# Two fill products between the row scores and the key scores of every step of a fused attention and Fourier kernel

## The chip, the cores and the metric

The kernel runs on one core of a Trainium2 chip. The metric is the device time of one execution in microseconds (us). Before the change three runs gave 2705.79, 2703.69 and 2701.54, with a median of 2703.69. A change within 0.2%, about 5.4 us, is what a measurement of this kernel can hardly tell from none.

## What is computed

```python
def _A_ref(x, wq, wk, wv, wo):          # S = 2048, D = 1024, 32 heads of 32
    q = (x @ wq).reshape(B, S, H, Dh).transpose(0, 2, 1, 3)
    k = x @ wk                          # one key and one value head for all 32
    v = x @ wv
    p = softmax(einsum("bhqd,bkd->bhqk", q, k) * Dh ** -0.5)
    o = einsum("bhqk,bkd->bhqd", p, v)
    return o.transpose(0, 2, 1, 3).reshape(B, S, H * Dh) @ wo

def _B_ref(x, seq_re, seq_im, hid_re, hid_im):
    a, b = x @ hid_re.T, x @ hid_im.T
    return seq_re @ a - seq_im @ b

out = concatenate([_A_ref(...), _B_ref(...)], axis=-1)
```

## The kernel before

The attention is cut into 32 units (four blocks of 512 queries, eight groups of four heads), and each unit into 32 steps. Step n of the main loop (line 940) does two things for attention. `score_step(n + 44)` (line 858) calls `scores` (line 744): two products of 512 columns, the **row scores** of a later unit, go into a tile `pss` (two buffers of two banks). VectorE takes the maximum of each row from it (`nm<-pss`), and in the next step `row_sums` (line 755) has ScalarE write the exponentials back over `pss` and read out their sum. `expo(n)` (line 805) makes two products of 512 columns, the **key scores** of the present unit, in `pst` (one buffer of two banks), and ScalarE writes their exponentials to a tile `p`. In the trace the row scores are `pss<-kst,qst`, the key scores `pst<-qst,kst`.

ScalarE's queue therefore holds, step by step, the row sum of the step before (an ACTIVATE and the READ_ACCUMULATOR) and then the exponential of this step's key scores. As `pst` has one buffer, the key scores of a step can begin only when the exponential of the step before has been read out; as `pss` has two, the row scores of a step need the row sum of two steps before.

All other matrix work (the projections, the Fourier half and the output projection, as three products of split operands each) is a long list of **fill products** `psb<-rh,mh`, `psb<-rl,mh`, `psb<-rh,ml` of 512 columns. `take(n)` (line 379) issues the next n of them; every product that `take` issues also moves the preparation on (`pump` and `run_later`), and the last one of a group (12 or 24 products) has its result taken out of PSUM, mostly by VectorE. Of the 5376 fill products a part runs in the prologue; `goal` (line 926) spreads the rest evenly over the steps, and `level(n)` (line 932) gives each step its share.

Steps 0, 12 and 22 of a unit (`ENDS`) are closed by a **burst**: `pv` (line 819) multiplies the collected `p` tiles by the values, 40 or 48 products `psb<-p,v` with 32 output rows each, four running side by side. `aside` (line 405) first issues up to five fill products when the fill group that is open has only begun or is nearly over. `level` leaves these steps out, and shares the work up to the next burst among the other steps:

```python
        if r in ENDS:
            return
        more = min(e for e in ENDS if e > r) - r
        left = goal(n + more) - pos["fill"]
        take(round(left / more))
```

In the last 44 steps there are no row scores left.

Of the kernel before, what the change touches and what calls it, by code (L numbers as in the profile page):

```python
# [101 lines left out]
def tile_kernel(ctx: ExitStack, tc, xT, wq, wkv, wo, xbT, wT, cT, out):  # L102
# [51 lines left out]
    class Line:  # L154
# [24 lines left out]
        def pump(self):  # L179
            for k in range(4):  # L180
                while self.may(k) and self.items[self.n[k]].due - self.lead[k] <= pos["fill"]:
                    self.step(k)
# [94 lines left out]
    def add(gs):  # L277

        for g in gs:
            i0 = g.at = end[0]  # L280
            end[0] += g.n
            if groups and g.set[0] is not groups[-1].set[0]:
                prev["set"] = prev["this"]
                prev["this"] = i0
            for c, it in enumerate(g.right):
                if it.need is None:
                    it.need = i0 + 3 * c
                    p0 = min(prev["set"], i0 - it.back)
                    it.due = min(it.need, p0 + (i0 - p0) * (g.first + c + 1) // (len(g.set) * len(g.right))) - it.ahead
                    RL.items.append(it)  # L290
                it.last = i0 + 3 * c + 2
            for c, it in enumerate(g.left):
                if it.need is None:
                    it.need = it.due = i0 + 12 * c
                    ML.items.append(it)
                it.last = i0 + 12 * c + 11
            for it in g.ys:
                it.due = i0 + g.n
                ylist.append(it)
            groups.append(g)  # L300
# [14 lines left out]
    def at(p, f):  # L315
        k = len(later)
        while k and later[k - 1][0] > p:
            k -= 1
        later.insert(k, (p, f))

    def run_later():
        while later and later[0][0] <= pos["fill"]:
            later.pop(0)[1]()
# [29 lines left out]
    def bank(name, open_=False):  # L353

        while held:
            held.pop(0)()
        b = 1 - cur["bank"] if cur["bank"] is not None else int(used[1] < used[0])
        cur["at"] += 1
        used[b] = cur["at"]
        if open_:  # L360
            cur["bank"] = b
        return ps_b[b].tile([P, W], F32, name=name)
# [10 lines left out]
    def product(g, ps, j):  # L373
        c, w = divmod(j, 3)
        l, r = g.left[c // 4], g.right[c]
        a = (l.lo if w == 2 else l.hi)[:, c % 4]
        te.matmul(ps[:g.rows], a, r.lo if w == 1 else r.hi, start=j == 0, stop=j == g.n - 1)

    def take(n):
        for _ in range(n):  # L380
            if cur["group"] >= len(groups):
                return
            g = groups[cur["group"]]
            j = pos["fill"] - g.at
            if j == 0:
                cur["ps"] = bank("psb", True)
            if j % 3 == 0:
                RL.force(g.right[j // 3])
            if j % 12 == 0:
                ML.force(g.left[j // 12])  # L390
            product(g, cur["ps"], j)
            pos["fill"] += 1
            if j == g.n - 1:
                cur["group"] += 1
                assert all(hasattr(it, "done") for it in g.ys)
                g.post(cur["ps"])
                cur["at"] += 1
                used[cur["bank"]] = cur["at"]
                cur["bank"] = None
                if g.ys:  # L400
                    at(pos["fill"] + 2 * BEHIND + 5, lambda n=len(g.ys): yused.__setitem__(0, yused[0] + n))
            pump()
            run_later()
# [174 lines left out]
    def wo_set(e):  # L578
        return [Item([(lambda g=g: wo[g * P:(g + 1) * P, e * W:(e + 1) * W], 1)]) for g in range(NG)]
# [90 lines left out]
    def o_group(b, t, e, ws):  # L670
        def post(ps):
            r0 = b * W + t * P
            to = out[r0:r0 + P, e * W:(e + 1) * W]
            if b < NQ - 1:
                oo = op.tile([P, W], F32, name="qh")
                dve.tensor_copy(oo, ps)
                store(to, oo)
                return

            n = len(halves)  # L680
            halves.append(n)
            oo = pp.tile([P, 2, W], F32, name="p")
            if n + 1 < 8:
                if n % 2:
                    dve.tensor_copy(oo[:, 0], ps)
                else:
                    act.activation(oo[:, 0], ps, AF.Copy)
                move(act, to, oo[:, 0])
                return
            for k, q in enumerate((act, sp)):  # L690
                cols = slice(k * W // 2, (k + 1) * W // 2)
                if k:
                    dve.tensor_copy(oo[:, k, :W // 2], ps[:, cols])
                else:
                    act.activation(oo[:, k, :W // 2], ps[:, cols], AF.Copy)
                move(q, to[:, cols], oo[:, k, :W // 2])
        return Group([o_left(b, t, q) for q in range(2)], ws, post)
# [101 lines left out]
    def inverse(u):  # L799
        rb[u] = onp.tile([P, W], F32, name="rb")  # L800
        for h in range(4):
            r = r_d[u][4 * h:4 * h + 4].rearrange("t c -> (t c)")
            sp.dma_start(rb[u][h * DH:(h + 1) * DH], r.unsqueeze(0).to_broadcast([DH, W]))

    def expo(n):
        u, r = divmod(n, SU)
        c, hp_ = divmod(r, 2)
        pt[u, c, hp_] = pp.tile([P, 2, W], F32, name="p")
        ps = ps_t.tile([P, 2, W], F32, name="pst")
        for a in range(2):  # L810
            te.matmul(ps[:, a], kst[:, c * P:(c + 1) * P], qst[u][:, 2 * hp_ + a], start=True, stop=True)
        act.activation(pt[u, c, hp_], ps, AF.Exp)
# [45 lines left out]
    def score_step(s):  # L858

        if s < total:  # L860
            u, r = divmod(s, SU)
            if r == SU - 6 and u + 1 < len(units):
                open_unit(u + 1)
        if SU <= s < SU * (len(units) + 1) and s % SU == TURN:
            row_sums(s - 1)
            lse_3((s - SU) // SU)
        if s < total:
            scores(s)
        row_sums(s - 1)
        u, e = divmod(s - SU, SU)  # L870
        if 0 <= u < len(units):
            for f in LSE.get(e, ()):
                f(u)
# [52 lines left out]
    def goal(n):  # L926
        return PRO + (FILL - PRO - LAST - MORE * (total - QUIET)) * n // total + MORE * max(n - QUIET, 0)
# [4 lines left out]
    def level(n):  # L932
        r = n % SU
        if r in ENDS:
            return
        more = min(e for e in ENDS if e > r) - r
        left = goal(n + more) - pos["fill"]
        take(round(left / more))

    for n in range(total):  # L940
        u, r = divmod(n, SU)
        if n == total - 12:
            w1 = wo_set(1)
            add([o_group(NQ - 1, t, e, ws) for e, ws in ((0, w0), (1, w1)) for t in range(4)])
        score_step(n + SU + LEAD)
        if ends:
            ends.pop(0)()
        expo(n)
        if r == 16:
            inverse(u)  # L950
        if r in ENDS and n:
            pv((n - 1) // SU, (ENDS.index(r) - 1) % (len(CUT) - 1))
        level(n)


    last = groups[len(groups) - 8:]
# [75 lines left out]
```

## Time and profile before

| what | value |
|---|---|
| three runs, median | 2703.69 us |
| the profiled execution's own time | 2701.05 us |
| its span, first to last instruction | 2699.3 us |
| granted TensorE clock, whole span | 1.0 |
| PE busy | 2691.8 us (100%), 13820 products |
| weight loads (PEld) | 1918.1 us (71%) |
| ScalarE | 2134.8 us (79%) |
| VectorE | 1592.8 us (59%) |
| GpSimd | 1723.7 us (64%) |
| DMA traffic | 538.24 MB, mean 199 GB/s |

Times are of one profiled execution; "busy" of PE counts pipelined products from issue to their modelled end, so two products that overlap share their time, and a short wait between products does not show in the share. The start times in the timeline do show it. "Idle before" names what ended a wait.

### The profile page before, as it was taken

The numbers are of one execution on the slowest core, as the hardware profiler recorded it, in microseconds if no ns is written. First come the engines' busy times: TensorE is split into PE (matmuls) and PEld (weight loads), VectorE is DVE, ScalarE is ACT, GpSimd is POOL, SyncE is SP. The second block draws the span as 40 slices with busy tenths as digits, with TensorE's granted clock in tenths as the row PEclk, the third lists the DMA queues.
The fourth block names the chain that finished last, engine by engine and source line by source line (L and its number), as shares of the span: only waits on it lengthen the run. The fifth ranks groups of instructions, "written<-read, shape, count | busy, mean of one in ns | idle before, by whom it ended". The sixth has DMA issues, their size and how long they took to land.

```text
span 2699.3 us, 40577 instructions
## 1 busy us (share of the span) xinstructions
PE 2691.8 (100%) x13820; PEld 1918.1 (71%) x13820; DVE 1592.8 (59%) x1826; ACT 2134.8 (79%) x3131; POOL 1723.7 (64%) x1711
## 2 busy tenths in 40 slices
PE   9999999999999999999999999999999999999999
PEld 6876767676777767677776777667677776767767
DVE  5766666666666666565565656666565555655411
ACT  3588888888888888888888888888888888888741
POOL 4854425777547558765556675576887987865751
PEclk9999999999999999999999999999999999999999
DMA  8543336887788566564354588984675765644665
GB/s 277 190 136 128 114 97 202 282 285 233 241 268 281 203 226 195 175 193 142 125 160 152 183 258 278 306 262 128 213 226 161 223 199 159 209 142 134 192 211 187
DMA packets 316931, 538.24 MB, mean 199 GB/s; under 512 B 35962, under 2 KB 63354, under 8 KB 316666
## 3 DMA queue, kind: packets, MB, share of 16 engines
q1 hardware_dynamic: 315572, 533.69, 61.6%
q8 instruction: 109, 1.79, 0.3%
q10 hardware_dynamic: 1152, 1.97, 0.2%
q14 instruction: 98, 0.80, 0.1%
HBM read 395.58 MB, written 138.15 MB: 198 GB/s over the span
## 4 chain that ended last, share of the span: by engine, by line
PE 99%; ACT 0%; DVE 0%; DMA 0%; SPq 0%; issue 0%; ACTq 0%
PE psb L79 62%; PE pss L79 19%; PE pst L79 18%; ACT pss L79 0%; DVE nm L79 0%; DMA p<-in_xT_dram 0%; ACT p L79 0%; SPq L79 0%; DVE y L79 0%; DVE qh L79 0%; DVE rl L79 0%; ACT rh L79 0%; DVE p L79 0%; ACTq L79 0%
## 5 line engine op out<-in xcount | busy, mean ns | idle before, releaser
L79 DVE TENSOR_REDUCE nm<-pss 128x1 f32<-128x1024 f32 x1024 | 1252.5, 1223 | 562.0 <-PE pss L79 561.3
L79 ACT ACTIVATE p<-pst 128x1024 f32<-128x1024 f32 x1026 | 1056.6, 1030 | 437.7 <-PE pst L79 425.1
L79 ACT ACTIVATE pss<-pss,nm 128x1024 f32<-128x1024 f32 x1024 | 1114.7, 1089 | 57.2 <-DVE nm L79 55.5
L79 PE MATMUL psb<-rh,mh 128*128 128x512 f32 x1790 | 698.2, 390 | 0.3 <-ACT rh L79 0.3
L79 PE MATMUL psb<-rl,mh 128*128 128x512 f32 x1790 | 697.8, 390 | 0.6 <-DVE rl L79 0.5
L79 PE MATMUL psb<-rh,ml 128*128 128x512 f32 x1790 | 697.7, 390 | 0.0
L79 PE MATMUL pss<-kst,qst 128*128 128x512 f32 x2048 | 641.5, 394 | 0.2
L79 PE MATMUL pst<-qst,kst 128*128 128x512 f32 x2048 | 641.0, 394 | 0.5 <-ACT p L79 0.3
L79 POOL TENSOR_TENSOR ml<-m,mh 128x512 fp32r<-128x512 f32 x366 | 473.5, 1294 | 35.1 <-ACT mh L79 26.2
L79 PEld LDWEIGHTS pss<-kst,qst 128*128 128x128 f32 x2048 | 377.9, 188 | 125.4 <-issue 51.1
L79 PE MATMUL psb<-p,v 128*32 128x512 f32 x4096 | 459.3, 594 | 0.0
L79 PEld LDWEIGHTS pst<-qst,kst 128*128 128x128 f32 x2048 | 375.0, 188 | 103.0 <-ACT p L79 27.0
L79 PEld LDWEIGHTS psb<-rh,mh 128*128 128x128 f32 x1790 | 336.0, 188 | 75.6 <-ACT rh L79 1.8
L79 PEld LDWEIGHTS psb<-rl,mh 128*128 128x128 f32 x1790 | 336.0, 188 | 73.7 <-DVE rl L79 1.9
L79 PEld LDWEIGHTS psb<-rh,ml 128*128 128x128 f32 x1790 | 336.0, 188 | 71.1
L79 POOL CAST mh<-m 128x512 fp32r<-128x512 f32 x365 | 224.5, 615 | 229.1 <-PE psb L79 211.9
L79 PEld LDWEIGHTS psb<-p,v 128*32 128x32 f32 x4096 | 123.3, 110 | 283.0 <-issue 275.2
L79 POOL TENSOR_TENSOR m<-m,m 128x512 f32<-128x512 f32 x220 | 284.4, 1293 | 54.5 <-DMA m<-o 19.6
L79 POOL TENSOR_TENSOR rl<-r,rh 128x512 fp32r<-128x512 f32 x208 | 269.2, 1295 | 4.0
L79 POOL CAST rh<-r 128x512 fp32r<-128x512 f32 x208 | 129.0, 620 | 194.2 <-PE psb L79 147.3
L79 ACT ACTIVATION_READ_ACCUMULATOR pss<-pss,nm 128x1 f32 x1024 | 212.5, 207 | 0.0
L79 POOL TENSOR_TENSOR r<-r,r 128x512 f32<-128x512 f32 x120 | 155.1, 1293 | 52.3 <-DMA r<-in_wT_dram 33.6
(92 smaller groups left out, 791.3 us busy)
## 6 DMA issues: line engine op xcount, KB each, us to landing
m<-in_cT_dram SPq DMA_DIRECT2D x384, 256.0 KB
r<-s SPq DMA_DIRECT2D x192, 256.0 KB
y<-y SPq DMA_DIRECT2D x128, 256.0 KB
r<-in_wT_dram SPq DMA_DIRECT2D x88, 256.0 KB
m<-in_xbT_dram SPq DMA_DIRECT2D x88, 256.0 KB
y<-u SPq DMA_DIRECT2D x80, 256.0 KB
m<-in_wq_dram SPq DMA_DIRECT2D x64, 256.0 KB
qst<-qh SPq DMA_DIRECT2D x64, 256.0 KB
```

The costliest lines, as they stand in the source:

```text
L79: return lambda *a, **k: self.tc.keep_in_program_order(f(*a, **k))
```

## The change

Before, a step issues row scores, key scores, the burst if there is one, and then its share of fill products. After, `level` returns the share and the loop issues up to two of its products between the row scores and the key scores, and the others where all of them stood. A step that a burst closes now has a share too, of two products.

```diff
     def level(n):
         r = n % SU
         if r in ENDS:
-            return
+            return 2
         more = min(e for e in ENDS if e > r) - r
         left = goal(n + more) - pos["fill"]
-        take(round(left / more))
+        return max(round(left / more), 0)
...
         score_step(n + SU + LEAD)
         if ends:
             ends.pop(0)()
+        fill = level(n)
+        first = min(fill, 2)
+        take(first)
         expo(n)
         if r == 16:
             inverse(u)
         if r in ENDS and n:
             pv((n - 1) // SU, (ENDS.index(r) - 1) % (len(CUT) - 1))
-        level(n)
+        take(fill - first)
```

PE's queue at a step that a burst closes, late in the program (`psb<-p,v` is the burst, listed here as 20 pairs of products). Before:

```order
L79 MATMUL psb<-rh,mh 128x512
L79 MATMUL pss<-kst,qst_758 128x512 x2
L79 MATMUL pst<-qst_2057,kst 128x512 x2
L79 MATMUL psb<-p,v 32x512 x20
L79 MATMUL pss<-kst,qst_758 128x512 x2
L79 MATMUL pst<-qst_2057,kst 128x512 x2
L79 MATMUL psb<-rl,mh 128x512
```

After:

```order
L79 MATMUL psb<-rh,mh 128x512
L79 MATMUL pss<-kst,qst_758 128x512 x2
L79 MATMUL psb<-rl,mh 128x512
L79 MATMUL psb<-rh,ml 128x512
L79 MATMUL pst<-qst_2057,kst 128x512 x2
L79 MATMUL psb<-p,v 32x512 x20
L79 MATMUL pss<-kst,qst_758 128x512 x2
L79 MATMUL psb<-rh,mh 128x512
L79 MATMUL psb<-rl,mh 128x512
L79 MATMUL pst<-qst_2057,kst 128x512 x2
```

Two fill products stand before the key scores of the closing step, which had none, and two before those of the step behind the burst.

PE's queue from the burst at step 460 on (step 12 of its unit), the start of a run of nine steps. Before:

```order
L79 MATMUL psb<-p,v 32x512 x24
L79 MATMUL pss<-kst,qst_758 128x512 x2
L79 MATMUL pst<-qst_2057,kst 128x512 x2
L79 MATMUL psb<-rh,ml 128x512
L79 MATMUL psb<-rh,mh 128x512
L79 MATMUL psb<-rl,mh 128x512
L79 MATMUL psb<-rh,ml 128x512
L79 MATMUL psb<-rh,mh 128x512
L79 MATMUL pss<-kst,qst_758 128x512 x2
L79 MATMUL pst<-qst_2057,kst 128x512 x2
L79 MATMUL psb<-rl,mh 128x512
L79 MATMUL psb<-rh,ml 128x512
```

After:

```order
L79 MATMUL psb<-p,v 32x512 x24
L79 MATMUL pss<-kst,qst_758 128x512 x2
L79 MATMUL psb<-rh,mh 128x512
L79 MATMUL psb<-rl,mh 128x512
L79 MATMUL pst<-qst_2057,kst 128x512 x2
L79 MATMUL psb<-rh,ml 128x512
L79 MATMUL psb<-rh,mh 128x512
L79 MATMUL pss<-kst,qst_758 128x512 x2
L79 MATMUL psb<-rl,mh 128x512
L79 MATMUL psb<-rh,ml 128x512
L79 MATMUL pst<-qst_2057,kst 128x512 x2
L79 MATMUL psb<-rh,mh 128x512
```

The step behind this burst had five fill products and has four, two on either side of the key scores. ScalarE's queue has the same order in both programs.

## Rows read from the trace of the kernel before

**Rows 1.** The page: the span, PE's busy time, and the chain by engine.

```profile
span 2699.3 us, 40577 instructions
PE 2691.8 (100%) x13820; PEld 1918.1 (71%) x13820; DVE 1592.8 (59%) x1826; ACT 2134.8 (79%) x3131; POOL 1723.7 (64%) x1711
...
PE 99%; ACT 0%; DVE 0%; DMA 0%; SPq 0%; issue 0%; ACTq 0%
```

**Rows 2.** The waits of the whole span: who for whom, us, times, longest.

```profile
ACT pss L79 <- DVE nm L79: 55.5, 62, 12.8
...
PEld pst L79 <- ACT p L79: 27.0, 108, 0.7
```

**Rows 3.** Timeline, PE, 1145 to 1158 us: start, length, instruction, how many in a row.

```profile
1145.43 0.61 PE L79 MATMUL pss<-kst,qst 128*128 128x512 f32 x2
...
1147.24 0.62 PE L79 MATMUL pss<-kst,qst 128*128 128x512 f32 x2
...
1149.34 0.62 PE L79 MATMUL pss<-kst,qst 128*128 128x512 f32 x2
...
1151.16 0.61 PE L79 MATMUL pss<-kst,qst 128*128 128x512 f32 x2
1151.64 0.73 PE L79 MATMUL pst<-qst,kst 128*128 128x512 f32 x2
...
1153.36 0.62 PE L79 MATMUL pss<-kst,qst 128*128 128x512 f32 x2
...
1155.21 0.61 PE L79 MATMUL pss<-kst,qst 128*128 128x512 f32 x2
...
1157.40 0.40 PE L79 MATMUL pss<-kst,qst 128*128 128x512 f32 x1
```

**Rows 4.** Timeline, ACT, the same stretch.

```profile
1148.55 1.03 ACT L79 ACTIVATE p<-pst 128x1024 f32<-128x1024 f32 x1
1149.45 1.10 ACT L79 ACTIVATE pss<-pss,nm 128x1024 f32<-128x1024 f32 x1
1150.45 0.22 ACT L79 ACTIVATION_READ_ACCUMULATOR pss<-pss,nm 128x1 f32 x1
1150.54 1.05 ACT L79 ACTIVATE p<-pst 128x1024 f32<-128x1024 f32 x1
...
1152.53 1.06 ACT L79 ACTIVATE p<-pst 128x1024 f32<-128x1024 f32 x1
```

**Rows 5.** Timeline, weight loads, the same stretch; in brackets the idle time before.

```profile
1151.64 0.30 PEld L79 LDWEIGHTS pst<-qst,kst 128*128 128x128 f32 x2 [0.28 <-ACT p L79]
```

**Rows 6.** Timeline, DVE, around 1700 us.

```profile
1699.03 0.69 DVE L79 COPY qh<-psb 128x512 f32<-128x512 f32 x1
1699.64 0.68 DVE L79 TENSOR_TENSOR y<-y,psb 128x512 f32<-128x512 f32 x1
1700.24 2.52 DVE L79 TENSOR_REDUCE nm<-pss 128x1 f32<-128x1024 f32 x2
```

**Rows 7.** Timeline, ACT, the same stretch.

```profile
1700.17 1.03 ACT L79 ACTIVATE p<-pst 128x1024 f32<-128x1024 f32 x1
1701.55 1.09 ACT L79 ACTIVATE pss<-pss,nm 128x1024 f32<-128x1024 f32 x1 [0.35 <-DVE nm L79]
```

**Rows 8.** Timeline, PE, the same stretch.

```profile
1699.51 0.62 PE L79 MATMUL pst<-qst,kst 128*128 128x512 f32 x2
...
1702.98 0.63 PE L79 MATMUL pss<-kst,qst 128*128 128x512 f32 x2
1703.72 0.73 PE L79 MATMUL pst<-qst,kst 128*128 128x512 f32 x2
```

**Rows 9.** Timeline, PE, one burst and the products on either side.

```profile
1314.65 0.61 PE L79 MATMUL pst<-qst,kst 128*128 128x512 f32 x2
1315.20 4.50 PE L79 MATMUL psb<-p,v 128*32 128x512 f32 x40
1319.63 0.73 PE L79 MATMUL pss<-kst,qst 128*128 128x512 f32 x2
```

## The prediction, on record before the run

> **What bounds the kernel now.** I read the page first. PE carries 99% of the chain that ended last and shows busy all through [rows 1], so the time is PE's products plus whatever PE waits between them. The busy share hides short waits; the starts in PE's timeline show them. In [rows 3] the row scores of successive steps start at 1145.43 and 1147.24, and eight products stand between: 1.81 us, or 0.2266 us a product. A step with five fill products (nine products) is then worth 2.04, one with four 1.81.
>
> The second view is ScalarE's timeline. In [rows 4] exponentials of key scores start at 1148.55, 1150.54 and 1152.53, 1.99 apart, and what lies between (the row sum, its read-out, the next exponential) follows without idle time. So ScalarE's own pace is 1.99 us a step. A five-product step just covers it; a four-product step is 0.18 too short. Then the key scores, whose tile has one buffer, meet an exponential that has not finished. The waits name it: 108 weight loads for key scores waited for ScalarE [rows 2].
>
> What that costs is in [rows 3]. Four- and five-product steps take turns there: 1.81, 2.10, 1.82, 2.20, 1.85, 2.19 us, against 1.81 and 2.04 without waits. The excess is 0, 0.06, 0.01, 0.16, 0.04, 0.15, together 0.42 for three four-product steps: **0.14 us for each**. It agrees with ScalarE's pace: a pair needs 3.98 and has 3.85 of products.
>
> A second cause is VectorE. At 1699.03 it takes two fill results out of PSUM, 0.69 and 0.68, and the next row maxima start only at 1700.24 [rows 6]. The row sum behind the exponential of 1700.17 begins 1.38 after it, having waited 0.35 for VectorE [rows 7], where it otherwise begins 0.90 after (1148.55 to 1149.45, [rows 4]). PE pays at 1703.72: the key scores start 0.74 after the row scores instead of 0.45, and the pair itself is 0.11 longer [rows 8].
>
> **The change, part by part.** PE's products stay the same in number and kind, so PE's floor is unchanged: 0. ScalarE's queue keeps its order: 0 from that.
>
> *Steps that a burst closes.* They get two fill products, and where those two leave a group just begun or nearly done, `aside` issues more. Counted in the built order over the 980 steps that have row scores beside them, closing steps held 149 fill products and now hold 325. The burst's own edges do not change: 0.55 from key scores to burst, 4.43 for 40 products, then the row scores [rows 9]. So these 176 products cost what they cost elsewhere, 176 x 0.2266 = 39.9 us, but they have left the ordinary steps. During a burst ScalarE has time to spare anyway, so they cover nothing there. What they covered before was ScalarE's 1.99.
>
> *Ordinary steps.* In the same count, six-product steps fall from 107 to 14, five-product steps go from 731 to 739, and four-product steps rise from **49 to 134**, in 46 runs between bursts instead of 25. The 85 added ones cost 0.14 each as in [rows 3]: 11.9 us. Bounds: the first four-product step of a run cost 0.06, so at least 85 x 0.06 = 5.1; the dearest pair cost 0.04 + 0.15 = 0.19, so at most 16.2. I take 0.14 because it is the mean over a run of the kind that is added, and ScalarE's pace gives the same.
>
> *The key scores, later in the step by two products (0.45 us).* From one step's key scores to the next nothing is gained, since both move. VectorE gains: the exponential, and the row sum queued behind it, come 0.45 later after the row scores, so a maximum that is late by the 0.48 of [rows 7] is all but hidden. Of the 108 waits, 49 four-product steps account for 33 to 98 (in [rows 3] two for three such steps, at most two each), which leaves 10 to 75 for VectorE, the opening steps and the last stretch without row scores. I take ten at 0.35 (a little less than the 0.29 + 0.11 of [rows 8], since that is a dear one): **-3.5**. Bounds: none, and 75 at 0.1, or -7.5. The wait that may come in its place is on PE again, in the row scores' tile: below.
>
> *What is queued behind.* Results taken out by VectorE, the casts on GpSimd and the loads on SP's queue are issued by `take`, product by product, so they keep their places among the fill products and move by at most two products against the attention. A result that falls due on one of the two moved products waits behind that step's maxima; with two fill buffers the next group is unhindered. 0.
>
> *Row scores.* The row sum that frees their tile is later by 0.45. Counted from a step's row scores, key scores now start at 0.91, the exponential 0.66 later (1699.51 to 1700.17, [rows 7, 8]), and the sum is read out 2.12 after that (1148.55 to 1150.67, [rows 4]): 3.69. The row scores two steps on start at 4.08 with five and five products, 3.85 with four and five. The slack falls from 0.85 to 0.39, and from 0.62 to 0.16. Key scores in a four-product step have less: the exponential ends at 0.91 + 0.66 + 1.03 = 2.60 and they start at 2.72. ScalarE's backlog holds up whichever comes first, and PE cannot be slowed below ScalarE's pace, which the 0.14 already holds. I take 0; bounds 0 and one longer pair (0.11) for each added step, 9.4.
>
> *Sum:* 11.9 - 3.5 = **+8.4 us**. The profiled execution took 2701.05, so 2709.45 for its like; it stands 2.64 under the median of 2703.69, so the median goes to **2712.1 us**.
>
> *A rule to weigh.* In [rows 5] the weight loads of a pair that waited begin only at 1151.64, after 0.28 idle behind ScalarE, at the start of the product itself, and the pair takes 0.73 where one that did not wait took 0.62 [rows 8]. The Trainium skill ("TensorE: Matmul & The Clock Gate", section "Step-by-step: what each phase is for") says that the next tile's weights are pulled ahead and load while the present matmul runs. By that rule a wait would cost its own length alone, the first four-product step of each run would be free, and the sum would be lower by 21 x 0.14 = 2.9: +5.5, still the forecast's case. The row disagrees and decides.
>
> **The rivals.**
> *Faster.* With VectorE out of the way, ScalarE might run faster than 1.99 a step. The point that decides is 1.93, half of a pair's 3.85: below it four-product steps cost nothing. Then the present 49 x 0.14 = 6.9 go, and the 3.5: -10.4, 2693.3. For it: 62 waits of row sums for VectorE, 55.5 us [rows 2]. Against it: in [rows 4] ScalarE waits for nobody and still takes 1.99.
> *No difference.* Added four-product steps are the cheap kind, 0.06: 5.1 - 3.5 = +1.6, 2705.3; with the larger relief -2.4, 2701.3. For it: 21 of the 85 are the first of their run. Against it: the other 64 are not.
> *Row scores wait as well.* +8.4 + 9.4, 2721.5, if the 0.16 of slack is eaten by the backlog and PE pays twice in a step. Against it: a PE that pays twice lets ScalarE catch up.
> That the change does not do what it says is ruled out by the built order.
>
> **How the numbers follow.** Forecast 0.59, no difference 0.27, row scores 0.07, faster 0.07. What a measurement of this kernel can tell from none is 0.2%, 5.4 us. The forecast's own range is +5.9 (0.11 a step) to +12.7 (0.19 a step), all slower; so slower 0.66, same 0.27, faster 0.07. The range runs from the no-difference case, 2702, to the forecast's upper end plus what runs scatter, 2719; the faster case and the row-score case are left out.
>
> **What would show it.** Right: waits of key scores for ScalarE rise from 108 to about 190 or more; key scores follow a two-fill gap; in runs of alternating four and five products ScalarE's exponentials start 1.99 apart and a pair of steps takes about 3.99; waits of row sums for VectorE fall; burst rows stay at 4.43. Wrong: exponentials closer than 1.93; a pair of such steps at 3.85; weight loads `pss` waiting for ScalarE by the hundred; or a burst that starts later than 0.55 after its key scores.

## The result: 2712.4 us, and the profile after

Seven runs of the changed kernel gave a median of 2712.41 us (2711.25 to 2713.16), and the kernel before, beside them, 2702.81 (2700.97 to 2705.79). The ratio is 1.0034, with a 95% interval of 1.0022 to 1.0046: slower, by 9.6 us. The forecast was 2712.1, slower by 8.4.

The page of the changed kernel, its span and its busy times, against [rows 1]:

```profile
span 2710.9 us, 40574 instructions
...
PE 2702.6 (100%) x13820; PEld 1905.1 (70%) x13820; DVE 1592.1 (59%) x1826; ACT 2118.8 (78%) x3131; POOL 1723.7 (64%) x1711
```

The number of products is the same, 13820, and PE is as "busy" as before. Of the 11.6 us by which the span is longer, 10.8 show up as PE time (2702.6 against 2691.8), although PE computes nothing more: the share counts a pair that waits as a longer pair.

The waits of the changed kernel, who for whom, against [rows 2] (us, times, longest):

```profile
ACT pss L79 <- DVE nm L79: 50.0, 45, 12.8
...
PEld pst L79 <- ACT p L79: 31.2, 170, 0.6
...
PEld pss L79 <- ACT pss L79: 23.1, 89, 0.3
```

Waits of key scores for ScalarE went from 108 to 170, and row sums wait for VectorE 45 times, where it was 62. The third row is nearly new: row scores wait for ScalarE 89 times. In the same view of the kernel before it reads

```profile
PEld pss L79 <- ACT pss L79: 0.8, 2, 0.5
```

One of the runs of steps that now alternate, in PE's timeline (start, length, instruction, how many in a row):

```profile
1277.67 0.74 PE L79 MATMUL pss<-kst,qst 128*128 128x512 f32 x2
...
1279.65 0.62 PE L79 MATMUL pss<-kst,qst 128*128 128x512 f32 x2
...
1281.56 0.73 PE L79 MATMUL pss<-kst,qst 128*128 128x512 f32 x2
...
1283.75 0.62 PE L79 MATMUL pss<-kst,qst 128*128 128x512 f32 x2
...
1285.60 0.70 PE L79 MATMUL pss<-kst,qst 128*128 128x512 f32 x2
...
1289.62 0.70 PE L79 MATMUL pss<-kst,qst 128*128 128x512 f32 x2
...
1293.64 0.70 PE L79 MATMUL pss<-kst,qst 128*128 128x512 f32 x2
```

From 1285.60 to 1289.62 and on to 1293.64, a four- and a five-product step take 4.02 us each time, where their seventeen products (nine fill products and eight of the scores) are worth 17 x 0.2266 = 3.85: 0.17 is lost per pair. This run is the one behind the burst at step 460. Before, seven of its nine steps had five products and two had six. ScalarE's exponentials in the same run:

```profile
1283.39 1.04 ACT L79 ACTIVATE p<-pst 128x1024 f32<-128x1024 f32 x1
...
1285.38 1.06 ACT L79 ACTIVATE p<-pst 128x1024 f32<-128x1024 f32 x1
...
1287.38 1.08 ACT L79 ACTIVATE p<-pst 128x1024 f32<-128x1024 f32 x1
...
1289.37 1.09 ACT L79 ACTIVATE p<-pst 128x1024 f32<-128x1024 f32 x1
```

They start 1.99 to 2.00 apart, as in [rows 4]: PE goes at ScalarE's pace here. The waits have moved, though: in [rows 3] and [rows 5] it was the key scores whose weight loads stood behind ScalarE, here it is the row scores. Their pair takes 0.70 to 0.73 instead of 0.62, and the weight loads of the dearest one:

```profile
1281.56 0.30 PEld L79 LDWEIGHTS pss<-kst,qst 128*128 128x128 f32 x2 [0.34 <-ACT pss L79]
```

As in [rows 5], they begin with the product itself, after an idle time that ScalarE ended.

One thing is new. Three bursts, at 505, 1615 and 1854 us, wait for VectorE (PE first, then VectorE, the same stretch):

```profile
1852.89 0.40 PE L79 MATMUL psb<-rh,ml 128*128 128x512 f32 x1
1853.93 1.49 PE L79 MATMUL psb<-p,v 128*32 128x512 f32 x12 [0.65 <-DVE qh L79]
```

```profile
1851.22 1.23 DVE L79 TENSOR_REDUCE nm<-pss 128x1 f32<-128x1024 f32 x1 [0.87 <-PE pss L79]
1852.36 0.27 DVE L79 TENSOR_REDUCE md<-nm 128x16 f32<-128x32 f32 x2
1852.55 0.40 DVE L79 TENSOR_REDUCE nm<-nm 128x16 fp32r<-128x32 f32 x2
1852.87 0.18 DVE L79 TENSOR_REDUCE l<-md 128x16 f32<-128x32 f32 x1
1853.08 0.25 DVE L79 RECIPROCAL nm<-l 128x16 f32<-128x16 f32 x1
1853.25 0.63 DVE L79 COPY qh<-psb 128x512 f32<-128x512 f32 x1
```

The burst starts 1.04 after the product ahead of it; in [rows 9] a burst starts 0.55 after the first product of a pair, so 0.32 after the second. Each of the three loses about 0.7, together 2.1 us. VectorE still had that step's row maxima and the unit's small reductions ahead of the COPY that frees a fill buffer. (At the other two it is an addition, `y<-y,psb`, behind the same reductions.)

### The profile page after: what moved, and what is told of

It is laid out like the page before. It is cut to its first block, busy times and chain, and to the rows that moved or that the text cites. A ratio compares the mean times of both kernels' runs of the same rounds, so it can differ in the third digit from the quotient of the medians.

```text
span 2710.9 us, 40574 instructions
## 1 busy us (share of the span) xinstructions
PE 2702.6 (100%) x13820; PEld 1905.1 (70%) x13820; DVE 1592.1 (59%) x1826; ACT 2118.8 (78%) x3131; POOL 1723.7 (64%) x1711
## 4 chain that ended last, share of the span: by engine, by line
PE 99%; DVE 0%; ACT 0%; DMA 0%; issue 0%; SPq 0%; ACTq 0%
PE psb L79 62%; PE pss L79 20%; PE pst L79 18%; DVE nm L79 0%; DMA m<-in_wq_dram 0%; ACT p L79 0%; DVE y L79 0%; ACT pss L79 0%; DVE qh L79 0%; ACT mh L79 0%; DVE md L79 0%; ACT rh L79 0%; DVE p L79 0%; SPq L79 0%; DVE l L79 0%
## 5 line engine op out<-in xcount | busy, mean ns | idle before, releaser
L79 DVE TENSOR_REDUCE nm<-pss 128x1 f32<-128x1024 f32 x1024 | 1252.1, 1223 | 541.0 <-PE pss L79 538.8
L79 ACT ACTIVATE p<-pst 128x1024 f32<-128x1024 f32 x1026 | 1065.0, 1038 | 471.9 <-PE pst L79 469.8
L79 ACT ACTIVATE pss<-pss,nm 128x1024 f32<-128x1024 f32 x1024 | 1123.5, 1097 | 50.1 <-DVE nm L79 50.0
L79 PE MATMUL psb<-rh,mh 128*128 128x512 f32 x1790 | 700.3, 391 | 0.2 <-ACT rh L79 0.2
L79 PE MATMUL psb<-rl,mh 128*128 128x512 f32 x1790 | 700.3, 391 | 0.0
L79 PE MATMUL psb<-rh,ml 128*128 128x512 f32 x1790 | 699.6, 391 | 0.0
L79 PE MATMUL pss<-kst,qst 128*128 128x512 f32 x2048 | 651.2, 399 | 0.0
L79 PE MATMUL pst<-qst,kst 128*128 128x512 f32 x2048 | 637.5, 392 | 0.2 <-ACT p L79 0.2
L79 POOL TENSOR_TENSOR ml<-m,mh 128x512 fp32r<-128x512 f32 x366 | 473.8, 1295 | 35.0 <-ACT mh L79 26.2
L79 PEld LDWEIGHTS pss<-kst,qst 128*128 128x128 f32 x2048 | 367.4, 188 | 145.0 <-issue 51.1
L79 PE MATMUL psb<-p,v 128*32 128x512 f32 x4096 | 459.4, 594 | 1.9 <-DVE y L79 1.3
L79 PEld LDWEIGHTS pst<-qst,kst 128*128 128x128 f32 x2048 | 370.6, 188 | 101.7 <-ACT p L79 31.2
L79 PEld LDWEIGHTS psb<-rh,mh 128*128 128x128 f32 x1790 | 336.7, 188 | 76.5 <-ACT rh L79 1.4
L79 PEld LDWEIGHTS psb<-rl,mh 128*128 128x128 f32 x1790 | 336.6, 188 | 75.6 <-issue 2.5
L79 PEld LDWEIGHTS psb<-rh,ml 128*128 128x128 f32 x1790 | 336.6, 188 | 72.3
L79 POOL CAST mh<-m 128x512 fp32r<-128x512 f32 x365 | 225.0, 616 | 242.3 <-PE psb L79 215.9
L79 PEld LDWEIGHTS psb<-p,v 128*32 128x32 f32 x4096 | 123.2, 110 | 285.3 <-issue 272.1
L79 POOL TENSOR_TENSOR m<-m,m 128x512 f32<-128x512 f32 x220 | 284.8, 1294 | 36.5 <-DMA m<-in_xbT_dram 16.8
L79 POOL TENSOR_TENSOR rl<-r,rh 128x512 fp32r<-128x512 f32 x208 | 269.4, 1296 | 4.0
L79 POOL CAST rh<-r 128x512 fp32r<-128x512 f32 x208 | 128.5, 618 | 198.2 <-PE psb L79 149.2
L79 ACT ACTIVATION_READ_ACCUMULATOR pss<-pss,nm 128x1 f32 x1024 | 222.8, 218 | 0.0
L79 POOL TENSOR_TENSOR r<-r,r 128x512 f32<-128x512 f32 x120 | 155.3, 1294 | 60.3 <-DMA r<-in_wT_dram 38.8
```

What stands on the lines that cost most here:

```text
L79: return lambda *a, **k: self.tc.keep_in_program_order(f(*a, **k))
```

## The experiments

The theory is the prediction's: the change gives fill products to steps that a burst closes, ordinary steps become too short for ScalarE's 1.99 us, and that costs; the place of the two products alone is a small gain. The rival: the place itself costs, because the row scores lose slack.

**The place alone, closing steps without fill products** (against the changed kernel):

```diff
         if r in ENDS:
-            return 2
+            return 0
```

> Two fill products stand between row and key scores in ordinary steps only; steps that a burst closes get none, so the count of four-product steps is 49 again. Theory (the 85 added four-product steps cost the time, at ScalarE's pace of 1.99 us; the place of the two products alone is a gain): 3.5 to 5 us under the kernel before, about 2698. Rival (the place costs, because the row scores' slack falls from 0.85 to 0.39 us): 6 to 10 us over it, about 2711.

Measured: 2727.37 us, 24 over the 2703.28 of the kernel before (ratio 1.0093, 1.0078 to 1.0109). Both expectations fail: the theory had about 2698, the rival about 2711. Key scores at the end of a run, in PE's timeline:

```profile
1323.68 0.62 PE L79 MATMUL pst<-qst,kst 128*128 128x512 f32 x2
1324.81 0.61 PE L79 MATMUL pss<-kst,qst 128*128 128x512 f32 x2
1325.41 0.73 PE L79 MATMUL pst<-qst,kst 128*128 128x512 f32 x2
1326.07 4.50 PE L79 MATMUL psb<-p,v 128*32 128x512 f32 x40
```

Key scores of the closing step come directly behind its row scores, those of the step before two products later than they used to. Between the two there are seven products, 1.59 us, and the exponential in between is not done. The pair starts 0.60 after the row scores, not 0.45, and takes 0.73, not 0.62: 0.26 in this closing step, and more where ScalarE is behind already. There are 91 such steps with row scores beside them, so 91 x 0.26 = 24 us or more. The gain of the ordinary steps stands against it, so the seam itself costs more than the 24 measured: about 29 against the kernel with the spacing kept, told below. So the place cannot be tried without a change of spacing in this way, and the two products of the closing step are what keeps the spacing in the changed kernel. The place with the spacing kept is tried below.

**The closing steps alone** (against the changed kernel):

```diff
-        first = min(fill, 2)
+        first = 2 if r in ENDS else 0
```

> Only steps that a burst closes get two fill products between their scores; in all others the products stay behind the key scores. Four-product steps number 134. Theory: the cost without the gain, 85 x 0.14 = 11.9 over the kernel before, about 2714.7, or 2 more if bursts wait for VectorE as in the change (three bursts, 0.7 each). Rival (the place costs): like the kernel before, 2703 to 2705.

Measured: 2715.51, 12.2 over the kernel before (1.0046, 1.0034 to 1.0059). That is near the theory's first figure, 11.9; but the same three bursts wait here too, so the theory's own figure for this kernel was 13.9, and the added steps come out cheaper than it said. The waits:

```profile
ACT pss L79 <- DVE nm L79: 53.6, 57, 12.8
...
PEld pst L79 <- ACT p L79: 46.4, 186, 1.1
...
PEld pss L79 <- ACT pss L79: 0.2, 1, 0.2
```

Here key scores do all the waiting, 186 times, and row scores wait for ScalarE once; yet it costs more than the change, not less. The 89 waits of row scores in the changed kernel are thus no cost on top of the key scores' waits. The two kernels differ in the place alone, so this is also a first test of the place: beside the closing steps' products it saves 2.6 us (12.2 less 9.6).

**Four products in closing steps** (against the changed kernel; two ahead of the key scores, two behind the burst):

```diff
-            return 2
+            return 4
```

> The change with four fill products in the steps that a burst closes, two ahead of the key scores and two behind the burst: four-product steps rise from 134 to 303. Theory: 169 x 0.14 = 23.7 over the change, about 2736. Rival (the place costs): like the change, 2712.

Measured: 2744.45, 32.0 over the changed kernel (1.0154 of the kernel before, 1.0141 to 1.0168). The direction and the order of size are the theory's, but each of the 169 further four-product steps costs 0.19, not 0.14. In the built order 63 of the four-product steps now follow another one directly, and there ScalarE has no five-product step to catch up in: 1.99 - 1.81 = 0.18 for each. That explains at most 63 x 0.04 = 2.5 of the 8.3 us between 23.7 expected and 32.0 measured. In the last stretch, without row scores, a single wait of PE for a load takes 1.2 more (`PE psb L79 <- DMA mh<-oh: 1.2, 1, 1.2`), which the trace of the changed kernel does not have; the rest stays open.

**The place alone, with the spacing kept** (against the kernel before, where `level` returns its count):

```diff
         score_step(n + SU + LEAD)
...
+        take(kept)
         expo(n)
...
-        level(n)
+        fill = level(n)
+        kept = min(fill, 2)
+        take(fill - kept)
```

> The kernel before with its two last fill products of every ordinary step kept back until the next step's row scores are issued. Key scores keep the spacing of the kernel before from step to step, also to the step that a burst closes (49 four-product intervals); row scores alone come two products earlier. Theory (the place is a gain when the spacing of key scores is kept; the first of these kernels lost because its closing step had two products fewer between its key scores and those before): about 5.3 under the kernel before, its gain in ordinary steps, so 2698. Rival (the place itself costs): 2705 or more.

Measured: 2698.42, against 2702.85 of the kernel before (0.9982, 0.9973 to 0.9991): 4.4 us less, where the theory had 5.3 and the rival a loss. The place is a gain.

**The same with at least five products in an ordinary step**, as long as there are row scores (`n < QUIET`):

```diff
-        return max(round(left / more), 0)
+        return max(round(left / more), 5 if n < QUIET else 0)
```

> The same with at least five products in every ordinary step, so no four-product interval between key scores. Theory: a further 49 x 0.14 = 6.9 less, about 2691. Rival (ScalarE's pace is not what the four-product steps pay for): no less than 2697.

Measured: 2691.33 (0.9955, 0.9943 to 0.9968), 11.5 under the kernel before and 7.1 under the one just told. The theory had 2691, the rival no less than 2697. This version beats both kernels. Its waits:

```profile
ACT pss L79 <- DVE nm L79: 50.3, 46, 12.6
...
PEld pst L79 <- ACT p L79: 7.8, 32, 0.7
...
PEld pss L79 <- ACT pss L79: 1.0, 3, 0.5
```

Of 108 waits of key scores 32 are left.

**Five products, with the first kernel's closing steps** (the first edit above and the `5 if n < QUIET`):

> As the first of these kernels, and an ordinary step issues at least five products, so that no four-product step is left (840 of five, 47 of six). Theory: the 49 x 0.14 = 6.9 go as well, 10 to 12 under the kernel before, about 2692. Rival (the place costs): no better than 2705.

Measured: 2718.18 (1.0057, 1.0044 to 1.0069). The expected 2692 fails for the same reason as in the first of these experiments: the closing steps are the same, with the same loss. Against that kernel's 2727.37 the four-product steps give 9.2 less, near the expected 6.9.

**ScalarE made faster, with the change and without it.** Its row sum runs over fewer columns; the rest of the softmax's sum is left out, and nothing else:

```diff
-        act.activation(ps, ps, AF.Exp, bias=nm[u][:, j, i:i + 1], accum_out=nm[u][:, 8 + j, i:i + 1])
+        act.activation(ps[:, :896], ps[:, :896], AF.Exp, bias=nm[u][:, j, i:i + 1], accum_out=nm[u][:, 8 + j, i:i + 1])
```

> The change, with ScalarE's row sum over 896 of each half row's 1024 columns: 128 of every 1024 scores are left out of the softmax's sums. ScalarE's pace per step falls by about 0.11, from 1.99 to 1.88, below the 1.93 of a pair of four- and five-product steps; PE's work is the same. Theory: the 134 four-product steps lose all but about 0.03 each, 134 x 0.11 = 14.7 less, about 2698, with the three bursts that wait for VectorE still there (2.1). Rival (the place costs, whatever ScalarE's pace): 2710 or more.

> The kernel before with the same 128 of every 1024 scores left out of the sums. Theory: 49 x 0.11 = 5.4 less, and up to 4 less because a faster ScalarE catches up with what VectorE's lateness costs, 2694 to 2698, so that the change and the kernel before differ by 4 us at most where they differ by 9.6. Rival: they still differ by 9.

Measured: with the change 2702.5 (0.9996 of the kernel before as it stands, 0.9987 to 1.0005), without it 2699.21 (0.9987, 0.9978 to 0.9996). Both are above what was expected (about 2698, and 2694 to 2698), but the two differ by 3.3 where they differed by 9.6, within the 4 that the theory allowed; with PE's work untouched, two thirds of the change's cost go when ScalarE is 0.08 us faster per step. Of the 3.3 that stay, about 2 can be the three bursts, which still wait. Exponentials and row scores of the change with the short sum, at the place of the alternating run above:

```profile
1282.14 1.03 ACT L79 ACTIVATE p<-pst 128x1024 f32<-128x1024 f32 x1
...
1284.05 1.03 ACT L79 ACTIVATE p<-pst 128x1024 f32<-128x1024 f32 x1
```

```profile
1280.57 0.63 PE L79 MATMUL pss<-kst,qst 128*128 128x512 f32 x2
...
1284.48 0.61 PE L79 MATMUL pss<-kst,qst 128*128 128x512 f32 x2
...
1288.38 0.63 PE L79 MATMUL pss<-kst,qst 128*128 128x512 f32 x2
```

ScalarE can now go at 1.91, and a pair of steps takes 3.91 instead of 4.02. It does not come down to 3.85. Per four-product step the short sum saved 9.9 / 134 = 0.074 with the change and 3.6 / 49 = 0.074 without it, not the 0.11 expected; the 3.6 has an interval of 1.1 to 5.9, so the second figure is rough. So about half of what such a step costs is ScalarE's pace; what stays fits the one buffer of the key scores, which ties each pair to the exponential before it however long ScalarE rests afterwards. A second buffer was not tried.

## Why the prediction was right, point by point

*Four-product steps, 11.9 us.* The closing steps alone cost 12.2. Of that 2.1 can be the bursts that wait, which the trace of that kernel has too, at the same three steps; then the 85 added steps cost 10.1, or 0.12 each instead of 0.14, inside the bounds of 0.06 and 0.19. The cause holds: remove the last four-product steps and 7.1 us go (6.9 were put on 49 x 0.14), speed ScalarE up and most of the difference goes. ScalarE's pace is not the whole cause, though: at a pace of 1.91, under the 1.93 below which the prediction had these steps cost nothing, about half of their cost stayed. That the 0.14 also followed from the pace alone was in part chance.

*VectorE's relief, -3.5.* The place alone, spacing kept, gave -4.4, and beside the closing steps' products -2.6; both lie between the bounds of none and -7.5. The traces agree with the mechanism: waits of row sums for VectorE fell from 62 to 45, in the change (55.5 to 50.0 us) and with the place alone. VectorE itself was not made faster, so that all of the gain comes this way is not shown.

*Row scores, 0.* They wait 89 times, far more than the prediction let one think: it named waits of `pss` by the hundred as a sign against it. Its sign for the key scores, 190 waits or more, was missed as well: they wait 170 times. The term was right all the same, for the reason it gave. A pair of steps runs at ScalarE's pace, and whether the row or the key scores are held up does not matter; in the kernel in which hardly any but key scores wait the time is higher. The rival in which PE pays twice is out.

*Closing steps and fill buffers, 0.* This term failed in small: "with two fill buffers the next group is unhindered" held for the fill products but not for the burst, which needs a buffer as well; a burst that starts late was one of the prediction's own signs of being wrong. Three bursts, all in the third closing step of a unit, where VectorE also has the unit's small reductions, lose 2.1 us. In each kernel whose closing steps get products from `level` (the change and three of the experiments) these three bursts wait; in none of the others does one of them, though two of those had such a wait at some other burst. That the reductions are what makes VectorE late is read from the trace; taking them away was not tried.

*The sum.* -4.4 and +12.2 make 7.8, and 9.6 were measured. The 1.8 between them is what the place saves less beside the closing steps' products, 2.6 instead of 4.4. It is within the uncertainty (the interval of the 4.4 alone is 2.4 to 7.3), and it stays open. The traces can be compared without the medians. From the first row scores of the main loop to the last, with the same products between them, PE takes 2404.1 us in the kernel before, 2417.3 with the closing steps alone and 2414.2 with the change: 13.2 and 10.1 more. About 2.3 of each is the three bursts. That leaves 10.9, or 0.13 for each added step, and -3.1 for the place: together +7.8 where the forecast has +8.4, and the bursts on top. (The two profiled executions differ by 11.7 in all, more than the medians do: 1.1 lies ahead of the main loop and 0.5 behind it.)

That the forecast came within 0.3 us is in part luck. The change cost 1.2 us more than forecast, and the kernel before measured 0.9 under the 2703.69 from which the forecast started. Within the change, cheaper steps were more than made up for by three bursts that nobody had counted.

*The weight-load rule.* By the Trainium skill ("TensorE: Matmul & The Clock Gate", section "Step-by-step: what each phase is for") the sum would have been +5.5. Measured were +9.6, and the weight loads of a waiting pair again begin with the pair's start, 1281.56, and the pair takes 0.73 instead of 0.62; here the rule did not hold for a load that waits for another engine.

## What to carry to other kernels

When a step's work on a busy engine just covers another engine's pace, giving a few instructions to places where that engine rests anyway makes the other places too short: compare the length of each step, not the mean, with the pace of the engine beside it. A producer with one buffer is timed by the distance from its last use to its next, so a reordering has to keep that distance in every step, those at the seams included; here the seam alone was worth about 29 us (2727.37 against 2698.42). A floor on the work of each step (five products) was worth more than the reordering, 7.1 us against 4.4.

## What the runs showed of the hardware

A pair of products whose first one waited for ScalarE costs about 0.11 us beyond the wait (0.73 against 0.62), since its weight loads, too, begin only then; this holds for key scores and row scores alike. ScalarE's step of exponential, row sum and read-out, 1.03, 1.09 and 0.21 long, repeats every 1.99 and not every 2.33, because each starts 0.10 to 0.13 before the one ahead has ended [rows 4]; leaving out 128 of 1024 columns in the sum took about 0.08 from the period (1.91).
